# Transposing q and k by DMA from the seventh unit on, in an attention and feed-forward kernel

## The chip, the cores and the metric

The kernel runs on one core of a Trainium2 chip. The metric is the device time of one execution in microseconds. Before the change the median of three runs is 475.96 us (475.83 to 476.86). The profile is of one execution of its own.

The core's engines run side by side, each through its own list of instructions in order: TensorE (PE; PEld is its weight load), VectorE (DVE), ScalarE (ACT), GpSimd (POOL) and SyncE (SP). SyncE only issues transfers here (SPq is its queue of them); POOL casts, and issues the stores of results while attention runs. TensorE writes into PSUM, of which this kernel uses all banks; the other engines copy from there into SBUF.

## The reference

Eight batches of twelve heads, 448 tokens, head size 64; then a gated feed-forward block over 3584 tokens. All in float32; the kernel casts to bf16 (q, k) and f16 (the rest) on the chip.

```python
scores = scale * np.matmul(q, k.transpose(0, 1, 3, 2)) - np.log(S)
attn = 1.0 / (1.0 + np.exp(-scores))
attn_out = np.matmul(attn, v)                       # (8, 12, 448, 64)
x = attn_out.transpose(0, 2, 1, 3).reshape(B * S, H * D)   # (3584, 768)
g = x @ w_gate                                      # 768 -> 1536
silu = g * (1.0 / (1.0 + np.exp(-g)))
return (silu * (x @ w_val)) @ w_out                 # 1536 -> 768
```

## The kernel before, in words

**Units.** A unit is four heads of one batch: 24 units, three to a batch, numbered i from 0; b = i // 3. A unit has two head pairs (pp = 0, 1), and a pair fills the 128 partitions with two heads of 64. Of the 448 tokens, 384 are the main part, loaded as 128 partitions of three tokens (s = 0, 1, 2; NS = 3); the last 64 are the tail, loaded for a whole batch at once.

**One unit, step by step.** (1) SyncE loads q, k and v of the four heads (`load_main`, L239; 393 KB each) and, per batch, the tails (`tails_batch`, L214 and L225). The tails of q and k share a buffer sqk, q in one half of the partitions and k in the other, which half is which alternating by batch. (2) POOL casts them (`cast_main`, `cast_tails`, L199; value tails to vbd, L276). (3) TensorE transposes, for each pair, three blocks of k, three of q and one of the tails, each 128x128, into one PSUM bank (`tr`, L336 and L338); VectorE copies 832 columns of it to qkT (L342) and the k tail in two 64x64 blocks onto the diagonal of a zeroed 128x128 buffer kbd (L348). (4) Scores: `burst` (L362) takes two (pair, chunk) steps of four matmuls; `burst_tail` (L376) takes the key tails of both heads of a pair in one matmul, which is why the k tail has to be block-diagonal. (5) ScalarE takes the sigmoid (L385). (6) `pv` (L398, L400) multiplies by v; VectorE copies the result to xT (L405), which is already the transposed input of the feed-forward block.

**Feed-forward.** Per batch, `f1` makes twelve gate and value blocks: six matmuls for ps_g, six for ps_v (L424), with the sigmoid on ScalarE (L430) and two products on VectorE (L434 writes t and frees the bank of ps_g, L440 writes hT). ps_g and ps_v share two PSUM banks (tag "G"). Per pair of batches `f2` makes the output, twelve matmuls to a block (L472, ps_o; ps_ol at the end). The transposes of `tr` and the blocks of `f2` share one PSUM bank (tag "TO").

**Order.** The main loop (L560 on) lists operations in the order in which the work should be preferred: in round i the loads of unit i+3, the casts of unit i+2, in four slices the scores of unit i and the transposes of unit i+1 (slices 1 and 2), between them `f1` and `f2`. Each carries an engine, an assumed duration, its inputs and the buffer slots that it takes and gives back. `list_schedule` (L47) then plays the list through: an engine that is free takes the first operation of a window of its own list (40 for PE, 8 for POOL, 1 for SP) whose inputs and slots are there, by the assumed times. What it finds is emitted in order of its start times, so every engine's order on the chip is fixed. The chip then waits by semaphores, by its own times. The weights are loaded in rounds 0 to 4: twelve loads of w_out last (L308), cast on POOL (L313); staging buffers (tag "st") are ten for all loads.

The lines on which the change bears most:

```python
    slots = {"A": 2, "TO": 1, "P": 1, "G": 2, "st": 10, "sqk": 2, "sv": 2, "q16": 2, "k16": 2, "qk16": 2,
             "v16": 3, "qkT": 4, "pt": 10, "xT": 14, "osb": 2}
...
        a = op("PE", 0.41, fpe, deps=casts_of(i, pp), take=["TO"], give=[x for o in casts_of(i, 0) for x in o.take] if pp else [])
        m = op("DVE", 0.59, fm, deps=[a], take=["qkT"])
        kd = op("DVE", 0.4, fk, deps=[a, m, R.get(("sct", i - 2))], give=a.take)
```

Of the kernel before, what the change touches and what calls it, by code (L numbers as in the profile page):

```python
# [125 lines left out]
def kernel(  # L126
# [17 lines left out]
    SM = 384  # L144
# [16 lines left out]
    slots = {"A": 2, "TO": 1, "P": 1, "G": 2, "st": 10, "sqk": 2, "sv": 2, "q16": 2, "k16": 2, "qk16": 2,  # L161
             "v16": 3, "qkT": 4, "pt": 10, "xT": 14, "osb": 2}
# [4 lines left out]
    NKB = 4  # L167
    kbd = [one.tile([128, 128], BF16, tag=f"kbd{i}", name=f"kbd{i}") for i in range(NKB)]
# [5 lines left out]
    for t in kbd:  # L174
        nc.vector.memset(t, 0.0)
# [29 lines left out]
    def tails_batch(b):  # L205
        def load_qk():
            T["sqk", b] = stg.tile([128, H, D], FP32, tag="sqk", bufs=2, name=f"sqk{b}")
        lo, hi = (q, k) if b % 2 == 0 else (k, q)

        def part(src, sl, first):  # L210
            def fn():
                if first:
                    load_qk()
                nc.sync.dma_start(out=T["sqk", b][sl],  # L214
                                  in_=src[b][:, SM:S, :].rearrange("h p d -> p h d"))
            return fn
        a = op("SP", 0.6, part(lo, slice(0, 64), True), take=["sqk"], nbytes=64 * H * D * 4)
        c = op("SP", 0.6, part(hi, slice(64, 128), False), deps=[], nbytes=64 * H * D * 4)
        R["sqk", b] = [a, c]

        def vpart(hp):
            def fn():
                if hp == 0:
                    T["sv", b] = stg.tile([128, H // 2, D], FP32, tag="sv", bufs=2, name=f"sv{b}")
                nc.sync.dma_start(out=T["sv", b][64 * hp:64 * hp + 64],  # L225
                                  in_=v[b][hp:H:2, SM:S, :].rearrange("h p d -> p h d"))
            return fn
        R["sv", b] = [op("SP", 0.6, vpart(0), take=["sv"], nbytes=64 * H // 2 * D * 4),
                      op("SP", 0.6, vpart(1), nbytes=64 * H // 2 * D * 4)]
# [16 lines left out]
    def cast_main(i, nm, eng, dt, part=None):  # L246
        def fn():
            if part in (None, 0):
                T[nm, i] = sb.tile([128, NS, 4, D], dt, tag=nm, bufs=slots["v16"] if nm == "v16" else 2,
                                   name=f"{nm}_{i}")  # L250
            h0, h1 = (0, 4) if part is None else (2 * part, 2 * part + 2)
            src = T["st_" + nm[0], i][:, h0:h1].rearrange("p h s d -> p s h d")
            cp(eng, T[nm, i][:, :, h0:h1, :], src)
        n = 4 if part is None else 2
        take = []
        if part in (None, 0):
            take = [nm]
        last = part in (None, 1)
        R[nm, i, part] = op(eng, 0.05 + n * 0.2, fn, deps=[R["st_" + nm[0], i, part]], take=take,
                            give=(R.get(("st_" + nm[0], i, None)) or R["st_" + nm[0], i, 0]).take if last else [])  # L260

    def cast_tails(i, eng="POOL"):
        b, r = divmod(i, QB)

        def fqk():
            T["qk16", i] = sb.tile([128, 4, D], BF16, tag="qk16", bufs=2, name=f"qk16_{i}")
            cp(eng, T["qk16", i], T["sqk", b][:, 4 * r:4 * r + 4, :])
        R["qk16", i] = op(eng, 0.4, fqk, deps=R["sqk", b], take=["qk16"], give=R["sqk", b][0].take if r == QB - 1 else [])
# [48 lines left out]
    def casts_of(i, pp):  # L317
        o = [R["qk16", i]]
        for nm in ("q16", "k16"):
# [346 lines left out]
```

## Time and profile before

| | |
|---|---|
| median of three runs | 475.96 us |
| profiled execution | 474.18 us, span 472.0 us |
| TensorE busy | 451.4 us (96%), 2832 matmuls |
| VectorE, ScalarE, POOL busy | 205.1 us (43%), 221.9 us (47%), 120.5 us (26%) |
| granted TensorE clock | 0.991 on average |
| transposes | 336 matmuls of 128x128 (L336: 288, L338: 48) |
| transfers | 58.66 MB, mean 124 GB/s; the queue of SP 51.13 MB, that of POOL 7.08 MB |

A row of the timeline or of the chain gives the start and the length in microseconds from the span's start, the engine, the line, and what is written from what; in square brackets stands how long the engine was idle before it and which event ended that. A row of the groups gives the count, then the total busy time and the mean nanoseconds of one, then the idle time just before. In a row of windows stand the stretch and its length, the busy time (and number of instructions) of PE, PEld, DVE, ACT and POOL, then the granted clock, the share of the DMA engines' time and the rate in GB/s. Matmuls are pipelined: the lengths of successive ones overlap, so that what one costs is read from the starts.

### The profile page before, as it was taken

Reading aid. Unit: us, or ns where it says so; the run is one execution under the profiler, and the core shown is the slowest. Engines: PE = TensorE matmul, PEld = TensorE weight load, DVE = VectorE, ACT = ScalarE, POOL = GpSimd, SP = SyncE. Lnnn points to the kernel's source line nnn. Section 1 sums busy time; section 2 is a strip of 40 time slices with the busy share of each in tenths; the row PEclk is TensorE's granted clock in tenths of the full one; section 3 lists DMA queues with packets and bytes.
Section 4 is the critical chain, followed back from the end, with each engine's and each line's share of the span. In section 5 each row is a group of like instructions: output and inputs, shape, how many; then the busy total and the mean of one; then the engine's idle time right before and its main releaser. Section 6 shows DMA issues by size and latency. Waiting matters only on the chain.

```text
span 472.0 us, 7257 instructions
## 1 busy us (share of the span) xinstructions
PE 451.4 (96%) x2832; PEld 224.0 (47%) x2832; DVE 205.1 (43%) x422; ACT 221.9 (47%) x296; POOL 120.5 (26%) x207
## 2 busy tenths in 40 slices
PE   2778999999999999999999999999999999999996
PEld 1323444444555545545455455454554544554563
DVE  2333655555544444444344453444544443335211
ACT  3577666656445354453554455445545344121111
POOL 4758768431211123121321232112210000000000
PEclk9979999999999999999999999999999999999999
DMA  8999999989413253332541323000000001110032
GB/s 213 347 300 357 320 334 365 235 224 293 120 34 102 67 135 78 93 115 69 134 126 60 101 72 96 0 35 35 33 28 7 35 35 33 55 47 0 35 101 100
DMA packets 68385, 58.66 MB, mean 124 GB/s; under 512 B 21248, under 2 KB 64512, under 8 KB 68352
## 3 DMA queue, kind: packets, MB, share of 16 engines
q1 hardware_dynamic: 66864, 51.13, 37.3%
q0 software_dynamic: 1488, 7.08, 4.2%
q8 instruction: 22, 0.36, 0.3%
q14 instruction: 11, 0.09, 0.1%
HBM read 47.19 MB, written 11.01 MB: 123 GB/s over the span
## 4 chain that ended last, share of the span: by engine, by line
PE 88%; DMA 7%; SPq 1%; DVE 1%; ACT 1%; POOL 0%; issue 0%
PE ps_g L424 23%; PE ps_v L424 22%; PE ps_o L472 18%; PE ps_sc L362 6%; PE ps_pv L398 6%; PE ps_ol L472 5%; PE ps_tr L336 3%; PE ps_pv L400 3%; DMA st_v<-in_v_dram 3%; DMA st_k<-in_k_dram 2%; DMA st_wv<-in_moe_w_val_dram 2%; PE ps_sct L376 2%; DVE t L434 1%; SPq L239 1%; ACT s L430 1%; PE ps_tr L338 0%
## 5 line engine op out<-in xcount | busy, mean ns | idle before, releaser
L385 ACT ACTIVATE pt<-ps_sc,sbiast 128x896 f16<-128x896 f32 x144 | 136.8, 1006 | 34.1 <-PE ps_sc L362 34.1
L424 PE MATMUL ps_g<-xT,wg 128*128 128x448 f16 x576 | 124.6, 352 | 1.1 <-DVE t L434 1.1
L424 PE MATMUL ps_v<-xT,wv 128*128 128x448 f16 x576 | 124.8, 353 | 0.0
L430 ACT ACTIVATE s<-ps_g 128x448 f16<-128x448 f32 x96 | 52.2, 544 | 146.6 <-PE ps_g L424 146.4
L434 DVE TENSOR_TENSOR t<-ps_g,s 128x448 f16<-128x448 f32 x96 | 59.9, 624 | 117.7 <-ACT s L430 117.7
L472 PE MATMUL ps_o<-wo,hT 128*128 128x384 f16 x516 | 90.9, 326 | 0.0
L472 PEld LDWEIGHTS <-hT 128*128 128x128 f16 x672 | 65.6, 98 | 45.8 <-issue 0.7
L424 PEld LDWEIGHTS <-wg 128*128 128x128 f16 x576 | 55.7, 98 | 53.3 <-issue 4.4
L440 DVE SCALAR_TENSOR_TENSOR hT<-ps_v,t 128x448 f16<-128x448 f32 x96 | 60.0, 625 | 43.3 <-PE ps_v L424 40.0
L424 PEld LDWEIGHTS <-wv 128*128 128x128 f16 x576 | 54.0, 98 | 45.8 <-issue 4.4
L405 DVE CAST xT<-ps_pv 128x448 f16<-128x448 f32 x48 | 29.9, 624 | 38.5 <-PE ps_pv L400 38.5
L362 PE MATMUL ps_sc<-qkT 64*128 64x448 bf16 x288 | 42.3, 369 | 4.3 <-ACT pt L385 3.6
L398 PE MATMUL ps_pv<-pt,v 128*64 128x448 f16 x288 | 37.8, 370 | 0.0
L199 POOL CAST v<-st_v 128x768 f16<-128x768 f32 (+1 forms) x25 | 20.2, 808 | 67.8 <-PE ps_pv L398 63.0
L497 POOL DMA_DIRECT2D out_dram<-osb x15 | 8.3, 556 | 100.0 <-DVE osb L485 53.0
L199 POOL CAST q<-st_q 128x768 bf16<-128x768 f32 x23 | 19.0, 825 | 58.2 <-issue 50.7
L342 DVE COPY qkT<-ps_tr 128x832 bf16<-128x832 bf16 x48 | 27.9, 582 | 11.5 <-PE ps_tr L338 11.5
L483 ACT ACTIVATE osb<-ps_o 128x384 f32<-128x384 f32 x22 | 10.8, 491 | 40.7 <-PE ps_o L472 40.7
L472 PE MATMUL ps_ol<-wo,hT 128*128 128x384 f16 x156 | 26.8, 326 | 0.0
L385 ACT ACTIVATE pt<-ps_sct,sbiast 128x896 f16<-128x896 f32 x24 | 24.1, 1003 | 4.2 <-PE ps_sct L376 4.1
L336 PE MATMUL ps_tr<-idn,k 128*128 128x128 bf16 x144 | 17.2, 233 | 8.6 <-ACT k L195 4.4
L485 DVE TENSOR_SCALAR osb<-ps_o 128x384 f32<-128x384 f32 x21 | 11.7, 558 | 27.3 <-PE ps_o L472 27.3
(36 smaller groups left out, 223.2 us busy)
## 6 DMA issues: line engine op xcount, KB each, us to landing
st_q<-in_q_dram SPq DMA_DIRECT2D x23, 384.0 KB, 4.8
st_k<-in_k_dram SPq DMA_DIRECT2D x23, 384.0 KB, 5.4
st_v<-in_v_dram SPq DMA_DIRECT2D x23, 384.0 KB, 6.3
out_dram<-osb POOLq DMA_DIRECT2D x15, 384.0 KB, 2.6
st_wg<-in_moe_w_gate_dram SPq DMA_DIRECT2D x12, 384.0 KB, 7.4
st_wv<-in_moe_w_val_dram SPq DMA_DIRECT2D x12, 384.0 KB, 8.5
st_wo<-in_moe_w_out_dram SPq DMA_DIRECT2D x12, 384.0 KB, 8.7
out_dram<-osb SPq DMA_DIRECT2D x8, 384.0 KB, 2.3
```

The source lines that it names most:

```text
L199: nc.gpsimd.tensor_copy(out=o, in_=i)
L336: nc.tensor.transpose(out=ps[:, off + s * 128:off + (s + 1) * 128], in_=src[:, s, hs, :], identity=idn)
L342: nc.vector.tensor_copy(out=m, in_=T["tr", i, pp][:, mo:mo + S + SM])
L362: nc.tensor.matmul(out=sc[:, hp, 0:S], lhsT=kT[r, s * 128:(s + 1) * 128], rhs=qT[r, :], start=True, stop=True)
L385: nc.scalar.activation(out=pt, in_=T[("sc",) + key][:, :, 0:S], func=SIGM, bias=sb_t, scale=qkscale)
L398: nc.tensor.matmul(out=ps[c, :], lhsT=T["v16", i][:, s, 2 * pp + hp, :], rhs=T["pt", i, pp, s][:, hp, :], start=(s == 0), stop=False)
L405: nc.vector.tensor_copy(out=t, in_=T["pv", i, pp])
L424: nc.tensor.matmul(out=ps, lhsT=w[c][:, j, ff * 128:(ff + 1) * 128], rhs=T["xT", b, j], start=(j == 0), stop=(j == KC - 1))
L430: nc.scalar.activation(out=t, in_=T["g", b, f], func=SIGM)
L434: nc.vector.tensor_tensor(out=t, in0=T["g", b, f], in1=T["s16", b, f], op=MULT)
L440: nc.vector.scalar_tensor_tensor(out=T["hT", m, f][:, o * S:(o + 1) * S], in0=T["v", b, f], scalar=HSC, in1=T["t1", b, f], op0=MULT, op1=MULT)
L472: nc.tensor.matmul(out=o, lhsT=T["hT", m, f][:, t * 128:(t + 1) * 128], rhs=wo16[f][:, cs], start=(f == 0), stop=(f == NF - 1))
```

## The change

The bf16 copies of q, k and their tails go into one buffer `src16` of two slots, 128 partitions x 2 pairs x 8 blocks x 128 columns: three blocks of k, a block of k tail, and four blocks of q with its tail (the tail first in odd batches). The k tail is written as two 64x64 pieces on the diagonal of its block, into a buffer zeroed once at the start, so that the transposed block is the block-diagonal key of `burst_tail`; kbd and its copies go. For that the k tails are loaded like the value tails, each head in its own half of the partitions, and a batch's tails take five loads where they took four. Each cast of q and k is of one pair (128x384) instead of both.

Units 0 to 5 are still transposed on TensorE: eight blocks a pair, then one VectorE copy of 1024 columns. From unit 6 (NPE = 6) `tr_dma` issues one transposing DMA from SyncE for the whole unit, SBUF to SBUF, 128 x 2048 bf16 into qkT as 16 transposed blocks. It is listed in round i, slice 2, for unit i+2. The planner is told 2.1 us on SP and 800000 bytes for it. qkT has three slots of a whole unit instead of four of a pair, given back by the unit's last `burst`. v is cast without reordering.

```diff
-    slots = {"A": 2, "TO": 1, "P": 1, "G": 2, "st": 10, "sqk": 2, "sv": 2, "q16": 2, "k16": 2, "qk16": 2,
-             "v16": 3, "qkT": 4, "pt": 10, "xT": 14, "osb": 2}
+    slots = {"A": 2, "TO": 1, "P": 1, "G": 2, "st": 10, "sq": 2, "sk": 2, "sv": 2, "src": 2,
+             "v16": 3, "qkT": 3, "pt": 10, "xT": 14, "osb": 2}
...
+    NSRC = slots["src"]
+    src16 = [one.tile([128, 2, 8, 128], BF16, tag=f"src{i}", name=f"src{i}") for i in range(NSRC)]
...
-    for t in kbd:
+    for t in src16:
         nc.vector.memset(t, 0.0)
...
+        for nm, src in (("sk", k), ("sv", v)):
+            R[nm, b] = [op("SP", 0.6, part(nm, src, 0), take=[nm], nbytes=64 * H // 2 * D * 4),
+                        op("SP", 0.6, part(nm, src, 1), nbytes=64 * H // 2 * D * 4)]
...
+    def cast_qk(i, nm, pp, eng):
+        g = groups(i // QB, nm)[0]
+
+        def fn():
+            o = src16[i % NSRC][:, pp, g:g + NS, :].rearrange("p s (h d) -> p s h d", h=2)
+            cp(eng, o, T["st_" + nm, i][:, 2 * pp:2 * pp + 2].rearrange("p h s d -> p s h d"))
...
+        R["c" + nm, i, pp] = op(eng, 0.43, fn, deps=[ld], take=["src"] if nm == "q" and pp == 0 else [],
+                                give=ld0.take if pp else [])
...
+        def fk():
+            for hp in range(2):
+                ps = slice(64 * hp, 64 * hp + 64)
+                cp(eng, src16[i % NSRC][ps, :, gk, ps], T["sk", b][ps, 2 * r:2 * r + 2, :])
...
+    def tr_pe(i, pp):
+
+        def fpe():
+            ps = T["tr", i, pp] = psum.tile([128, 8 * 128], BF16, tag="TO", bufs=1, name="ps_tr")
+            for g in range(8):
+                nc.tensor.transpose(out=ps[:, g * 128:(g + 1) * 128],
+                                    in_=src16[i % NSRC][:, pp, g, :], identity=idn)
...
+    def tr_dma(i):
+
+        def fn():
+            qkT_tile(i)
+            nc.sync.dma_start_transpose(
+                out=T["qkT", i].rearrange("p a (g c) -> p (a g) c", c=128),
+                in_=src16[i % NSRC].rearrange("p a g c -> p (a g c)"))
+        d = op("SP", 2.1, fn, deps=[R["c" + nm, i, pp] for nm in "qk" for pp in range(2)] + R["tails", i],
+               take=["qkT"], give=R["cq", i, 0].take, nbytes=800000)
+        R["qkT", i, 0] = R["qkT", i, 1] = d
...
     def casts(i):
-        cast_main(i, "q16", "POOL", BF16)
-        cast_main(i, "k16", "POOL", BF16)
+        for nm in "qk":
+            for pp in range(2):
+                cast_qk(i, nm, pp, "POOL")
         cast_tails(i)
-        cast_main(i, "v16", "POOL", FP16)
+        cast_v(i, "POOL")
         cast_vtail(i)
...
-                        if i + 1 < NQ:
-                            tr(i + 1, 0)
+                        if i + 1 < NPE:
+                            tr_pe(i + 1, 0)
...
+            if att and sl == 2 and NPE <= i + 2 < NQ:
+                tr_dma(i + 2)
```

Three places show how the order of the instructions moves. The first is on TensorE in the long middle of the kernel, behind the tail scores of a unit. Before (k_13, q_13 and qk_13 are the casts of unit 13):

```order
L376 LDWEIGHTS kbd_73
L376 MATMUL ps_sct<-qkT_1_2196,kbd_73 128x448
L336 LDWEIGHTS k_13_1949
L336 MATMUL ps_tr<-idn,k_13_1949 128x128
...
L336 MATMUL ps_tr<-idn,q_13_1943 128x128
...
L338 MATMUL ps_tr<-idn,qk_13_1964 128x128
L424 LDWEIGHTS wv_0_96
L424 MATMUL ps_v<-xT_0_1787,wv_0_96 128x448
```

Now:

```order
L392 LDWEIGHTS qkT_1858
L392 MATMUL ps_sct<-qkT_1858 128x448
L439 LDWEIGHTS wv_1_93
L439 MATMUL ps_v<-xT_0_1687,wv_1_93 128x448
L439 MATMUL ps_v<-xT_1_1733,wv_1_93 128x448
```

Three transposes of k, three of q and one of the tails have gone from between the tail scores and the value matmuls; the same goes for the second group of each unit. TensorE has 96 transposes in all where it had 336.

The second is on TensorE behind unit 5 (v_5), where the first unit transposed by DMA is read (qkT_987). The xT tiles up to xT_5_525 (before) and xT_5_512 (now) belong to batch 0, xT_0_642 to xT_5_1028 to batch 1. Before, one gate and one value group stand between the last scores of unit 5 (qkT_1_797) and the first of unit 6 (qkT_0_921):

```order
L362 MATMUL ps_sc<-qkT_1_797 128x448
L424 LDWEIGHTS wg_2_94
L424 MATMUL ps_g<-xT_0_279,wg_2_94 128x448
...
L424 MATMUL ps_v<-xT_5_525,wv_2_98 128x448
L362 LDWEIGHTS qkT_0_921
L362 MATMUL ps_sc<-qkT_0_921 128x448
L398 LDWEIGHTS v_5_717
L398 MATMUL ps_pv<-pt,v_5_717 64x448
```

Now:

```order
L413 MATMUL ps_pv<-pt,v_5_708 64x448
L415 MATMUL ps_pv<-pt,vbd_76 128x448
...
L439 MATMUL ps_v<-xT_0_256,wv_3_95 128x448
...
L439 MATMUL ps_g<-xT_5_512,wg_3_91 128x448
...
L439 MATMUL ps_v<-xT_5_512,wv_3_95 128x448
L439 LDWEIGHTS wg_0_88
L439 MATMUL ps_g<-xT_0_642,wg_0_88 128x448
...
L439 MATMUL ps_g<-xT_5_1028,wg_0_88 128x448
L377 LDWEIGHTS qkT_987
L377 MATMUL ps_sc<-qkT_987 128x448
```

Between the last ps_pv of unit 5, which stood behind the scores of unit 6, and those scores there are now four value groups and four gate groups on end. From the tail scores of unit 5 to the first scores of unit 6 TensorE's order is: one ps_sct, then seven pairs of value and gate groups, and between them two groups of scores and two ps_pv groups.

The third is SyncE at the end of the weight loads. Before (sqk and sv are tails, st_q, st_k and st_v the units' main loads):

```order
L308 DMA st_wo_990<-in_moe_w_out_dram 128x768
L308 DMA st_wo_1008<-in_moe_w_out_dram 128x768
L239 DMA st_q_1015<-in_q_dram 128x4x192
L239 DMA st_k_1028<-in_k_dram 128x4x192
L239 DMA st_v_1052<-in_v_dram 128x4x192
L214 DMA sqk_1063<-in_k_dram 64x12x64
```

Now:

```order
L324 DMA st_wo_958<-in_moe_w_out_dram 128x768
L324 DMA st_wo_973<-in_moe_w_out_dram 128x768
L357 DMA_TRANSPOSE qkT_987<-src_72 128x16x128
L231 DMA st_q_1013<-in_q_dram 128x4x192
L231 DMA st_k_1018<-in_k_dram 128x4x192
L231 DMA st_v_1032<-in_v_dram 128x4x192
L357 DMA_TRANSPOSE qkT_1036<-src_73 128x16x128
L209 DMA sq_1060<-in_q_dram 64x12x64
```

The transpose of unit 6 stands behind the twelfth load of w_out, ahead of the main loads of unit 8; that of unit 7 behind those. From there on one transpose stands ahead of the main loads of each following unit.

On POOL the q and k tails of a unit (406 ns a unit before, cast whenever they were there, often before q) now stand behind the two q casts, and the k tails of most units behind the two k casts.

150 lines of the change are left out of this document (65 added, 85 removed).

## The prediction

> **What bounds the kernel now.** I read the windows first (busy time of each engine by stretch), because an average over 472 us hides the stages; then TensorE's timeline, then the waits and transfers around the place where the first transposing DMA would stand.
>
> ```profile
> core 0: us, PE busy (x) PEld busy (x) DVE busy (x) ACT busy (x) POOL busy (x), PEclk, DMA share, GB/s
> 30.00:42.00 12.00, 9.54 (x53) 3.90 (x53) 3.62 (x9) 8.20 (x10) 8.98 (x13) 0.72 1.08 357
> 60.00:80.00 20.00, 20.00 (x134) 9.08 (x133) 10.47 (x22) 13.86 (x19) 14.34 (x24) 1.00 1.04 362
> 140.00:380.00 240.00, 240.00 (x1542) 120.80 (x1540) 109.84 (x224) 117.77 (x158) 46.16 (x84) 1.00 0.24 70
> 420.00:441.00 21.00, 19.91 (x101) 9.70 (x100) 9.99 (x16) 4.35 (x8) 0.00 (x0) 1.00 0.05 20
> ```
>
> There are three stages. Up to about 42 us TensorE waits for data (9.54 of 12 us busy). From 42 us TensorE has no gap, while VectorE and ScalarE are busy under half of the long stretch (110 and 118 of 240 us); until about 106 us the transfers are saturated too (share 1.04). So after 42 us a microsecond less on TensorE is a microsecond off the end, unless something new makes it wait. Where it transposes, it does this:
>
> ```profile
> 219.65 0.54 PE L376 MATMUL ps_sct<-qkT,kbd 128*128 128x448 bf16 x2
> 220.03 0.33 PE L336 MATMUL ps_tr<-idn,k 128*128 128x128 bf16 x3
> 220.20 0.33 PE L336 MATMUL ps_tr<-idn,q 128*128 128x128 bf16 x3
> 220.37 0.22 PE L338 MATMUL ps_tr<-idn,qk 128*128 128x128 bf16 x1
> 220.42 1.30 PE L424 MATMUL ps_v<-xT,wv 128*128 128x448 f16 x6
> ```
>
> Starts, not durations, give the cost, since matmuls overlap: 220.42 - 220.03 = 0.39 us for seven transposes, 0.056 us each.
>
> **Term 1, the transposes removed.** Units 6 to 23 are 18 units of two groups: 36 x 0.39 = 14.04 us off TensorE. (The Trainium skill, "TensorE: Matmul & The Clock Gate", Part 4, gives about 275 ns for one transpose within a kernel; by that 252 of them would be worth 69 us. The starts above say 0.056 us, and the sum goes by them.) VectorE loses the copies behind them, an engine with cover: nothing.
>
> **Term 2, one more transpose a group in units 0 to 5.** Eight where there were seven: 12 x 0.056 = +0.67 us, charged in full though part of it falls in the idle first 42 us.
>
> **Term 3, two-buffer stalls.** While the planner waits for the first transposed unit it pulls feed-forward work (ps_g, then ps_v) ahead, and in the new order three more gate products follow a gate/value pair with nothing between. Such a neighbourhood is at the end of the profile now:
>
> ```profile
> 420.34 1.30 PE L424 MATMUL ps_g<-xT,wg 128*128 128x448 f16 x6
> 422.93 1.29 PE L424 MATMUL ps_g<-xT,wg 128*128 128x448 f16 x6 [0.16 <-DVE t L434]
> 42.46 1.14 PE ps_v L424 x6
> ```
>
> A pair then takes 422.93 - 420.34 = 2.59 us, where two groups of 1.14 (third row, from the chain of waits) take 2.28: the gate waits for VectorE's t to free its bank. 3 x 0.31 = +0.93 us.
>
> **Term 4, POOL in the first 42 us.** POOL's casts are cut in halves, and the tails are cast after q rather than beforehand.
>
> ```profile
> L199 POOL CAST q<-st_q 128x768 bf16<-128x768 f32 x23 | 19.0, 825 | 58.2 <-issue 50.7 <-DMA st_q<-in_q_dram 6.9 <-DVE qkT L342 0.4
> L199 POOL CAST k<-st_k 128x384 bf16<-128x384 f32 x1 | 0.5, 510 | 0.0
> L199 POOL CAST qk<-sqk 128x256 bf16<-128x256 f32 x23 | 9.3, 406 | 8.7 <-DMA sqk<-in_k_dram 5.7 <-PE ps_sc L362 1.5 <-PE ps_g L424 0.8
> L276 POOL CAST vbd<-sv 64x128 f16<-64x128 f32 x48 | 14.0, 292 | 2.2 <-DMA sv<-in_v_dram 0.9
> ```
>
> A unit's q, k and tails cost 825 + 825 + 406 = 2.06 us now; then 4 x 0.51 + 0.41 (a q tail of 256 elements) + 2 x 0.29 (two k tails of 128) = 3.03 us: about +1 us a unit. After 42 us POOL has room for that (14.3 of 20 us busy, and a unit takes over 11). Before, TensorE waits for just these casts:
>
> ```profile
> 39.85 0.83 POOL L199 CAST q<-st_q 128x768 bf16<-128x768 f32 x1 [0.38 <-DMA st_q<-in_q_dram]
> 41.01 0.83 POOL L199 CAST k<-st_k 128x768 bf16<-128x768 f32 x1 [0.33 <-DMA st_k<-in_k_dram]
> 41.90 0.34 PE L336 MATMUL ps_tr<-idn,k 128*128 128x128 bf16 x3
> 53.03 0.54 PE L376 MATMUL ps_sct<-qkT,kbd 128*128 128x448 bf16 x2
> ```
>
> Unit 4 by the new order: q halves and q tail 39.85 + 1.02 + 0.41 = 41.3, k halves to 42.3, k tails to 42.9. TensorE, which would start these transposes at 41.90, starts at 42.9, but has moved a group of scores (0.49 us) ahead: it loses about 0.6. I take +0.7 (bounds: 0, if the transfer and not POOL is late, and 2, one microsecond each for units 3 and 4).
>
> **At no cost: zeroing and one more load.** The zeroed buffers grow from 64 columns (of four bytes) to 1024:
>
> ```profile
> L175 DVE MEMSET kbd<- 128x64 uint32 x4 | 0.3, 112 | 0.8 <-PEq L650 0.8
> L177 DVE MEMSET vbd<- 128x128 uint32 x3 | 0.4, 165 | 0.0
> 3.23 0.42 DVE L197 CAST q<-st_q 128x384 bf16<-128x384 f32 x1 [1.65 <-DMA st_q<-in_q_dram]
> ```
>
> By 0.83 ns a column (165 less 112 over 64) each takes 0.9 us, two 1.8; with the three of vbd VectorE is done at about 3.1 us, and the first load lets it begin at 3.23. If that cover is short, the start is late by the rest, a few tenths. A batch's tails take five loads instead of four, one more issue of about 0.63 us on SyncE (the tail row in term 5), within its slack.
>
> **Term 5, the first transposing DMA.** Unit 6 stands on SyncE behind the last w_out load, and TensorE's new order reaches its scores with no slack planned. When is it there, and when does TensorE ask?
>
> ```profile
> 64.63 0.54 PE L376 MATMUL ps_sct<-qkT,kbd 128*128 128x448 bf16 x2
> 68.76 5.18 SPq L308 DMA_DIRECT2D st_wo<-in_moe_w_out_dram x6
> 80.05 3.19 POOL L313 CAST wo<-st_wo 128x768 f16<-128x768 f32 x4
> 83.64 0.83 POOL L199 CAST q<-st_q 128x768 bf16<-128x768 f32 x1 [0.41 <-DMA st_q<-in_q_dram]
> ```
>
> TensorE: unit 5's tail scores (ps_sct) start at 64.63; add 0.7 (term 4) and four longer groups since unit 3 (0.22): 65.5. From there the new order has seven gate/value pairs (15.96), one ps_sct (0.38), two score groups (0.98), two ps_pv groups (1.96) and term 3 (0.93): it asks at **85.8 us**. The transfer: the last w_out load is there when its cast starts at about 82.4, and the load behind it landed at 83.6. In that load's place the transpose lands at 82.4 + X, X being its service time. It moves 128 x 2048 bf16 = 524 KB in 256-byte pieces.
>
> ```profile
> 171.00:172.00 1.00, 1.00 (x9) 0.44 (x9) 0.56 (x1) 0.00 (x0) 0.00 (x0) 1.00 1.08 362
> 173.00:174.00 1.00, 1.00 (x7) 0.49 (x5) 0.62 (x1) 0.00 (x0) 0.00 (x0) 1.00 1.37 167
> L214 SPq DMA_DIRECT2D sqk<-in_k_dram x2: 612/628/644, 170.2 to 229.1; - x2
> DMA to landing us min/median/max: 6.3/6.4/6.6
> ```
>
> No row shows a transposing DMA. Lower bound: the best rate of plain loads, 362 GB/s: X = 1.45 us. Nearest row: the tail loads, whose pieces are 256 bytes too, 167 GB/s: X = 3.1. Upper bound: a tail load of 197 KB takes 6.4 us from issue to landing; scaled by bytes (2.67), X = 17. I take 3.1, for the equal piece: landing at 85.5, before 85.8. Stall 0; it would be X - 3.4 us for a larger X.
>
> After unit 6 the slack grows: TensorE takes about 11.6 us a unit (53.03 to 64.63), then nearly 20 (from the ps_sct below, at 199.93, to the one at 219.65). A transpose waits for the buffer that the scores of three units earlier leave, so it may start nearly two units ahead: 20 to 35 us to spare. Behind it on SyncE wait the loads of q, k and v two units on; they have those two units. On POOL the casts two units on now wait for this transfer, since there are two source buffers; behind them stand that unit's v and value tails, which are read a unit later still.
>
> ```profile
> 199.93 0.54 PE L376 MATMUL ps_sct<-qkT,kbd 128*128 128x448 bf16 x2
> ```
>
> **The sum.** -14.04 + 0.67 + 0.93 + 0.7 + 0 = -11.7 us. The profiled execution took 474.18 us (span 472.0 and 2.2 around it) and would take 462.4; the median of the runs shown is 475.96, and minus 11.7 gives **464.2 us**.
>
> **The rivals.** (a) *Transposes of middling speed*, X from 4 to 8 us: only the saturated stretch suffers, TensorE stalls 0.6 to 5 us at units 6 to 10, and the end is at 465 to 469 us. For it: transposed writes have no row at all. Against: 256-byte pieces already run at 167 GB/s.
>
> (b) *Slow transposes, the other side*: each holds the transfers so long that units fall due faster than they arrive. Unit 10 is the fifth: it lands at 82.4 + 5X plus twelve main loads and a set of tails between (5.3 MB at 362 GB/s, 14.7), that is 97.1 + 5X, and is asked for at 85.8 + 4 x 11.6 = 132.2. The stall, 5X - 35, eats the gain of 11.7 from X = 9.4 on. At the upper bound, 17, a unit costs 17 + 3.8 us of transfers, so unit 23 lands at 82.4 + 17 + 17 x 20.8 = 453, and 89 us of work follow its first scores, which start at 382.92 in a span of 472.0:
>
> ```profile
> 382.92 0.55 PE L362 MATMUL ps_sc<-qkT 64*128 64x448 bf16 x4
> ```
>
> That is 542 us, or 544 with what lies around the span. For it: the tail loads' landing time; against: that time is mostly waiting behind two plain loads issued just before. (The Trainium skill, "VectorE: DVE Perf Modes", section "The three transpose paths", gives 1309 ns for one 128x128 block by DMA against 390 by TensorE, which speaks against this change: sixteen blocks one after another would be an estimated 21 us, and the chain above then ends near 615 us. No run here shows it yet; if blocks overlap, the figure is a latency and no rate.)
>
> (c) *The start costs more*: POOL, 9 of 12 us busy before 42 us, frees staging buffers later, loads start later, and TensorE's gapless run begins 3 to 6 us later: 467 to 470 us.
>
> (d) *It does not do what it says*: TensorE's freed time turns into waits for ScalarE or VectorE, and the time stays at 476. Both under half busy over 240 us speak against it.
>
> **How the numbers follow.** Forecast 0.62, (a) 0.16, (c) 0.08, (b) 0.11, (d) 0.03. The measurement can tell 0.2%, about 1 us, from no change. Faster are the forecast, (a) and (c): 0.86; same is (d): 0.03; slower is (b): 0.11. The range: below, 461.5, all of term 1 and little of the others; above, 470, where (a) and (c) end; (b) and (d) stay outside. The forecast alone: 462 to 466.
>
> **What would show it.** In the changed profile: transposes by DMA landing 2 to 5 us after their issue where transfers are idle; TensorE's windows from 140 us on still full, with no L336 rows; TensorE's idle time before unit 6's scores below 1 us; the first gapless window starting less than 1.5 us later. What would make it wrong: a landing time over 9 us, a TensorE wait for qkT that recurs from unit to unit, or a start that moves by more than 3 us.

## The result, and the profile after

The changed kernel takes **464.4 us** in the median of four runs (463.3 to 465.1) beside 475.9 of the kernel before on the same chip, a ratio of **0.976 (0.973 to 0.978)**. Run again beside later experiments it took 462.4 us, 0.974 (0.971 to 0.976). Forecast were 464.2 us and a range of 461.5 to 470. The profiled execution took 463.31 us, with a span of 461.2.

The windows of the changed kernel, in the stretches shown of before (the last one 11 us earlier, since the end has moved):

```profile
30.00:42.00 12.00, 8.03 (x42) 3.27 (x38) 2.63 (x4) 5.97 (x7) 8.93 (x16) 0.59 1.04 338
60.00:80.00 20.00, 20.00 (x123) 8.72 (x121) 10.36 (x17) 12.55 (x16) 14.14 (x27) 1.00 0.99 301
140.00:380.00 240.00, 240.00 (x1421) 116.01 (x1419) 93.76 (x152) 121.26 (x164) 51.76 (x117) 1.00 0.40 105
409.00:430.00 21.00, 19.91 (x102) 9.63 (x99) 9.98 (x17) 4.35 (x8) 0.00 (x0) 1.00 0.05 20
```

The long stretch is as full as before, with 1421 matmuls where there were 1542: TensorE's freed time did not turn into waits. The transfers' share there rose from 0.24 to 0.40. Only the first row is worse: 8.03 us busy of 12 where it was 9.54.

TensorE's timeline behind the tail scores of a unit has no transposes any more, and the value product follows at once:

```profile
197.13 0.54 PE L392 MATMUL ps_sct<-qkT 128*128 128x448 bf16 x2
197.51 1.30 PE L439 MATMUL ps_v<-xT,wv 128*128 128x448 f16 x6
```

The transposing DMAs, by their line, first between 75 and 130 us, then from 135 us on (nanoseconds of the issue on SyncE, least, median and most; then microseconds from the issue to the landing). The eighteenth lies between, at 131.16: it holds SyncE for 2.82 us and lands after 4.3.

```profile
L357 SPq DMA_TRANSPOSE qkT<-src x6: 4211/4586/6834, 78.9 to 122.8; - x6
DMA to landing us min/median/max: 6.3/6.9/8.8
...
L357 SPq DMA_TRANSPOSE qkT<-src x11: 1778/1981/3180, 148.1 to 331.4; - x11
DMA to landing us min/median/max: 4.3/4.3/4.9
```

Where transfers are idle, sixteen blocks are in place 4.3 us after the issue, which is at most 0.27 us a block. (The Trainium skill, "VectorE: DVE Perf Modes", section "The three transpose paths", gives 1309 ns for one block by DMA. As a rate the trace disagrees, with at most 270 ns a block for a whole unit in one instruction: its blocks overlap, or each takes less. One block alone was not measured here.)

**A clock inside the program.** Where the tail scores of unit 5 start splits the program well. These rows are of the changed kernel, then of the same kernel run again:

```profile
67.71 0.54 PE L392 MATMUL ps_sct<-qkT 128*128 128x448 bf16 x2
```

```profile
67.36 0.54 PE L392 MATMUL ps_sct<-qkT 128*128 128x448 bf16 x2
```

From there to the end it is 461.2 - 67.71 = 393.5 us, and 461.0 - 67.36 = 393.6 in the second execution. Five experiments below that alter tail loads and casts, of later batches too, and leave TensorE's order behind the point as it is, have 393.4 to 393.5. The kernel before has 472.0 - 64.63 = 407.4, and the experiment that alters only its loads 407.5. So in these traces the part behind it differs by 0.2 us at most, and nearly all the scatter of the runs is in the beginning. The span of every timed execution is known. If the constant holds in all of them, span less constant gives where the point lay in each, with far more executions than there are traces (the bounds are two standard errors; the twenty are of the changed kernel, in two sets of four, and of three experiments with the same beginning, each with its own constant):

| executions | unit 5's tail scores start at | rest |
|---|---|---|
| 47 of the kernel before | 65.4 +- 0.2 us | 407.4 |
| 20 with the changed kernel's beginning | 67.7 +- 0.5 us | 393.5 (changed kernel) |

The change in two numbers: **-13.9 us** behind that point and **+2.3 us** ahead of it. The second is less sure than its bound says. The changed kernel alone lies at 68.7 in its first four executions and at 66.7 +- 0.7 in the four run beside later experiments, while the kernel before stays within 65.2 to 65.6 in each of its four sets; and the experiment with four transposes a unit, which begins in the same way and is not among the twenty, lies at 69.0.

One rival can be tested on these executions. The granted clock in the window from 30 to 42 us fell too, from 0.72 to 0.59, and a slower TensorE would also start later. But at like clocks the gap stays: where the clock averages 0.99 or more over the span, the point lies at 65.3 (40 of the 47) and at 67.3 (10 of the 20); where it is lower, at 66.0 and 68.1.

The experiments take the two numbers apart.

### The profile page after: what moved, and what is told of

The parts are those of the page before. It is cut to its first block, busy times and chain, and to the rows that moved or that the text cites. A ratio compares the mean times of both kernels' runs of the same rounds, so it can differ in the third digit from the quotient of the medians.

```text
span 461.2 us, 6749 instructions
## 1 busy us (share of the span) xinstructions
PE 437.8 (95%) x2592; PEld 211.4 (46%) x2592; DVE 177.1 (38%) x290; ACT 221.1 (48%) x296; POOL 139.4 (30%) x299
## 4 chain that ended last, share of the span: by engine, by line
PE 87%; DMA 4%; SPq 4%; DVE 1%; ACT 1%; POOL 1%; issue 1%; POOLq 0%
PE ps_g L439 24%; PE ps_v L439 22%; PE ps_o L487 18%; PE ps_sc L377 6%; PE ps_pv L413 6%; PE ps_ol L487 5%; PE ps_pv L415 3%; SPq L216 2%; DMA st_wv<-in_moe_w_val_dram 2%; SPq L231 2%; PE ps_sct L392 2%; DMA st_v<-in_v_dram 2%; DVE t L449 1%; ACT s L445 1%; POOL src L199 1%; DMA st_q<-in_q_dram 1%
## 5 line engine op out<-in xcount | busy, mean ns | idle before, releaser
L199 POOL CAST src<-st_q 128x384 bf16<-128x384 f32 x46 | 22.0, 505 | 46.9 <-DMA st_q<-in_q_dram 41.9
L199 POOL CAST src<-st_k 128x384 bf16<-128x384 f32 x47 | 22.5, 506 | 6.2 <-DMA st_k<-in_k_dram 5.0
L377 PEld LDWEIGHTS <-qkT 64*128 64x128 bf16 x288 | 9.1, 95 | 32.5 <-issue 30.5
L500 DVE TENSOR_SCALAR osb<-ps_o 128x384 f32<-128x384 f32 x21 | 11.7, 558 | 30.7 <-PE ps_o L487 30.7
```

The costliest lines, as they stand in the source:

```text
L199: nc.gpsimd.tensor_copy(out=o, in_=i)
L377: nc.tensor.matmul(out=sc[:, hp, 0:S], lhsT=kT[r, s * 128:(s + 1) * 128], rhs=qT[r, :], start=True, stop=True)
L500: nc.vector.tensor_scalar_mul(T["osb", m, t][:, c], o, HREC)
```

## The experiments

### Where the gain is: transposes back on TensorE

**All units on TensorE.** The buffers, loads and casts of the changed kernel, without any transposing DMA.

```diff
-    NPE = 6
+    NPE = 24
```

> All 24 units are transposed on TensorE, from the same source buffer and with the same casts and loads as in the changed kernel; no transposing DMA. Theory A (the gain is TensorE's time for the transposes, 8 x 0.056 us a group): 36 groups x 0.45 = 16 us more than the changed kernel's 464.4, less up to 0.9 for the three two-buffer stalls that the old order does not have: 479.5 to 480.4, that is slower than the kernel before. Rival B (the gain comes from what went with the transposes: VectorE's diagonal copies, the free PSUM bank, the new layout): 464 to 470.

479.3 us, 1.009 (1.007 to 1.012): slower than the kernel before, as theory A has it. By the point above: 477.5 - 68.15 = 409.4 us behind it, 15.9 more than with DMAs from unit 6 on, or 0.44 us for each of 36 groups of eight. Rival B falls for the new layout and the missing diagonal copies, which stay here: the part behind the point is 2.0 us longer than in the kernel before, and 36 more transposes of 0.057 us make 2.0. The PSUM bank is taken again in this run, so it does not test what a free bank brings; the sums of starts further below leave about 0.5 us for that and all else.

**Units 6 to 11 on TensorE.**

```diff
-    NPE = 6
+    NPE = 12
```

> Units 6 to 11 go back to TensorE, units 12 to 23 stay with transposing DMAs, so that none stands in the saturated stretch. Theory A: 12 groups x 0.45 = 5.4 us more, less 0.9 if the three stalls at unit 6 go away: 468.8 to 469.8. Rival C (the transposes in the saturated stretch cost something that the trace does not show as a wait, 1 to 3 us): 466 to 468.

467.6 us, 0.984 (0.981 to 0.987), a little under what A expected (468.8), and within rival C's figures too; the time alone does not decide. The trace does: 464.5 - 66.14 = 398.4 us behind the point, 4.9 more than 393.5. A's 5.4 less what the three stalls cost (0.96, below) is 4.5. By C it would be another 1 to 3 us less, and it is 0.4 more, so C falls.

### How far the transposes are from costing something

**Each transpose issued twice.** The added one writes a buffer that nobody reads; the other engines' orders stay.

```diff
             qkT_tile(i)
+            nc.sync.dma_start_transpose(out=scr.rearrange(...), in_=src16[i % NSRC].rearrange(...))
             nc.sync.dma_start_transpose(
```

> Every transposing DMA is issued twice, first into a scratch buffer that nobody reads, then into qkT; the order on every other engine stays. Theory S (a transpose costs its transfer, X about 1.7 to 3 us, with slack after unit 6): X doubles to 3.4 to 6, TensorE stalls 2 to 4 us at unit 6 and no more after unit 10: 464 to 468. Rival Q (it costs the time that SyncE is held by the issue, 6.8 us for the first and 4.2 for the next five while transfers are saturated): unit 6 about 6.5 us late, units 7 to 10 fall behind by another 1 to 2 us each: 471 to 477. The prediction's formula for slow transposes, 5X - 35, gives a loss only from X = 7 on.

464.9 us, 0.978 (0.974 to 0.981), as theory S has it. SyncE's timeline, and TensorE's wait at unit 6:

```profile
77.11 6.90 SPq L359 DMA_TRANSPOSE scr<-src  x1
84.12 1.58 SPq L362 DMA_TRANSPOSE qkT<-src  x1
...
88.51 0.55 PE L382 MATMUL ps_sc<-qkT 64*128 64x448 bf16 x4 [1.68 <-DMA qkT<-src]
```

The first transpose holds SyncE for 6.9 us, the second, right behind it, for 1.58. So the long issue is a wait behind the saturated transfers and no price of the instruction; at the next four units the second ones take 1.86 to 2.86 us. A second one adds its transfer, and TensorE waits 1.68 us. Rival Q falls. The unit takes 1.6 us more and nothing is lost after it (461.5 - 66.41 = 395.1 behind the point, 1.6 over 393.5).

**Each transpose issued four times**, three of them into one buffer, so that each waits for the last to land.

```diff
+            for x in range(3):
+                nc.sync.dma_start_transpose(out=scr.rearrange(...), in_=src16[i % NSRC].rearrange(...))
```

> Every transposing DMA is issued four times, three of them into one scratch buffer, so that each of these waits for the one before to land (4.3 us or more): X about 16 us a unit. By the formula of the prediction's slow case: unit 23's transpose lands at 82.4 + 16 + 17 x (16 + 3.8) = 435, the end comes 89 us later, 524 us and 2 around the span: 526, within 20. If the slow case does not exist (SyncE and the transfers have room for four): below 480.

540.3 us, 1.137 (1.133 to 1.140). The slow case exists, 14 us further out than expected. The formula's stall at unit 10 was 5 x 16 - 35 = 45 us. Its tail scores start at 182.48 here and at 139.87 in the changed kernel; less the 1.4 us by which this execution began later (its unit 5 at 69.07), the stall is 41 us. The real transposes are issued from 94.64 to 423.42 us, 19.3 us apart (assumed 19.8); with the X of 15.5 that this gives, the formula's stall is 43.

```profile
94.64 2.57 SPq L362 DMA_TRANSPOSE qkT<-src  x1
...
423.42 3.07 SPq L362 DMA_TRANSPOSE qkT<-src  x1
```

What the formula lacked is seen in the windows and in the row of busy times:

```profile
90.00:140.00 50.00, 28.05 (x139) 11.19 (x141) 11.24 (x18) 17.23 (x23) 7.73 (x18) 0.78 0.89 180
380.00:440.00 60.00, 60.00 (x356) 29.03 (x354) 23.47 (x38) 30.27 (x42) 11.55 (x26) 1.00 0.77 158
```

```profile
PE 452.3 (84%) x2592; PEld 214.6 (40%) x2592; DVE 177.1 (33%) x290; ACT 221.2 (41%) x296; POOL 138.5 (26%) x299
```

The last transposes no longer set the end: TensorE is without a gap from 380 us, still working off what it had waited for. And in the stretch where it waits, its granted clock is lower (0.78, with 28 of 50 us busy): the same 2592 matmuls are busy for 452.3 us, against 437.8 in the changed kernel. How the 14 us divide between the two is not worked out.

**DMA from unit 3 on.**

```diff
-    NPE = 6
+    NPE = 3
```

> Units 3, 4 and 5 are transposed by DMA too. Theory A alone (TensorE's time): 6 groups x 0.45 = 2.7 us less than the changed kernel, 460 to 462. If a transpose in the saturated stretch holds SyncE for 4 to 7 us and the loads behind it as long: units 3 to 6 each start 4 to 7 us later than they could, of which the freed 0.9 us a unit pays little: 470 to 485, with TensorE waiting for loads and qkT between 30 and 90 us.

472.6 us, 0.996 (0.993 to 0.999): most of the gain is gone, as the second theory has it. Its transposes up to 95 us, and the first wait for one:

```profile
L357 SPq DMA_TRANSPOSE qkT<-src x5: 4225/7130/8118, 42.5 to 94.9; - x5
DMA to landing us min/median/max: 6.3/9.7/11.7
...
51.73 0.55 PE L377 MATMUL ps_sc<-qkT 64*128 64x448 bf16 x4 [3.47 <-DMA qkT<-src]
```

The first ones hold SyncE for over 7 us while weights and the next units' loads stand behind. TensorE is busy 13.64 of 18 us from 42 to 60 us, and 14.59 of 20 from 80 to 100. Unit 3's tail scores come 13 us later than in the changed kernel (56.15 for 42.99), of which the order makes up some later. Transfers are saturated here as they are for units 6 to 10. That these three units are not covered because TensorE has little other work so early is argued from the order, and no run tests it.

### What the start lost

POOL casts of unit 3's q and TensorE's first transposes behind them, in the changed kernel (the rows of POOL, then TensorE's):

```profile
30.62 0.95 POOL L199 CAST src<-st_q 128x384 bf16<-128x384 f32 x2 [0.60 <-DMA st_q<-in_q_dram]
31.64 0.40 POOL L199 CAST src<-sq 64x256 bf16<-64x256 f32 x1
32.10 0.64 POOL L199 CAST src<-sk 64x128 bf16<-64x128 f32 x2
33.15 0.95 POOL L199 CAST src<-st_k 128x384 bf16<-128x384 f32 x2 [0.41 <-POOL src L199]
...
33.71 1.03 PE L341 MATMUL ps_tr<-idn,src 128*128 128x128 bf16 x8 [2.54 <-POOL src L199]
```

The same place in the kernel before:

```profile
28.82 0.82 POOL L199 CAST q<-st_q 128x768 bf16<-128x768 f32 x1 [0.84 <-DMA st_q<-in_q_dram]
29.94 0.83 POOL L199 CAST k<-st_k 128x768 bf16<-128x768 f32 x1 [0.30 <-DMA st_k<-in_k_dram]
...
30.83 0.50 PE L336 MATMUL ps_tr<-idn,k 128*128 128x128 bf16 x3 [0.80 <-POOL k L199]
```

The transposes are 2.9 us later for two reasons: q arrives 1.8 us later, and from its cast to the transposes it is 3.1 us where it was 2.0. The second is POOL, foreseen in term 4. The first is a load, and in both kernels POOL waits for it. What makes the loads late? SyncE's timeline of the changed kernel has the tails of the second batch as follows, and issues unit 3's q at 26.64 (23.71 before):

```profile
18.39 0.61 SPq L209 DMA_DIRECT2D sq<-in_q_dram  x1
19.58 3.23 SPq L216 DMA_DIRECT2D sk<-in_k_dram  x2
22.85 3.69 SPq L216 DMA_DIRECT2D sv<-in_v_dram  x2
26.64 0.56 SPq L231 DMA_DIRECT2D st_q<-in_q_dram  x1
```

I had two theories: the one more load (H1), or that q and one half of k now share half of the partitions (H2).

**Tails of q and k loaded as before**, k's cast from its half onto both diagonal blocks.

```diff
-        for nm, src in (("sk", k), ("sv", v)):
+        def kpart():
+            r = slice(64, 128) if b % 2 == 0 else slice(0, 64)
+            nc.sync.dma_start(out=T["sq", b][r], in_=k[b][:, SM:S, :].rearrange("h p d -> p h d"))
...
-                cp(eng, src16[i % NSRC][ps, :, gk, ps], T["sk", b][ps, 2 * r:2 * r + 2, :])
+                kr = slice(64, 128) if b % 2 == 0 else slice(0, 64)
+                cp(eng, src16[i % NSRC][ps, :, gk, ps], T["sq", b][kr, 4 * r + hp:4 * r + 4:2, :])
```

> The tails of q and k are loaded as in the kernel before (one buffer, q in one half of the partitions, k in the other, four loads a batch); the k tails are cast from that half onto both diagonal blocks, with the same number of casts. POOL's work stays. Theory H2 (the 2.9 us that the start lost come from tail loads that put three quarters of the bytes of q's and k's tails into one half of the partitions): the start comes back by 2.5 to 2.9 us, unit 3's tail scores near 40.2 instead of 42.99, time 461.5 to 462. Theory H1 (they come from the one more load that SyncE issues, 0.63 us each): 463.1 to 463.8. POOL theory (term 4 of the prediction): 464.4, start unchanged.

462.3 us, 0.973 (0.971 to 0.976). The time lies between what H2 and H1 wrote down and decides nothing: both were reckoned from 464.4, and the changed kernel itself took 462.4 when it was run again (below). Unit 3's q is cast at 29.61, 1.0 us earlier, and the point behind unit 5 lies at 66.8 +- 0.7 over five executions, 0.9 us (0 to 1.8) earlier than the 67.7 of the table. Unit 3's tail scores start at 40.92, where six traces with the changed kernel's beginning have 41.60 to 43.26. By the point H2's 2.5 to 2.9 us do not come; it is near H1 (0.6 to 1.3).

**The kernel before, with k's tail in two loads** into the same half.

```diff
-        c = op("SP", 0.6, part(hi, slice(64, 128), False), deps=[], nbytes=64 * H * D * 4)
-        R["sqk", b] = [a, c]
+        R["sqk", b] = [a] + [op("SP", 0.6, half(hi, slice(64, 128), h0), nbytes=64 * H // 2 * D * 4)
+                             for h0 in (0, H // 2)]
```

> The kernel before with one edit: the k tail of a batch is loaded in two loads of six heads, into the same half of the partitions as before, so five tail loads a batch as in the changed kernel, but the halves stay even. H2: the start moves by 0.2 to 0.8 us, time 476.0 to 476.8. H1: the start moves by 2 to 3 us as in the changed kernel, 478 to 479.

476.1 us, 1.003 (1.001 to 1.004); the point lies at 66.6 +- 0.3 over twelve executions, 1.2 us later than in the kernel before, more than one issue of 0.63 us and less than H1 wrote down. The time alone lies in H2's range, but only because the kernel before took 474.7 us beside this run and not 475.96. H2's mechanism falls: the halves are even here, and unit 3's q is issued at 26.47 all the same. What one more load does shows in the windows from 4 to 12 us, behind the first batch's tails. First the kernel before, then with its k tail split, then the changed kernel, then with four tail loads again:

```profile
4.00:12.00 8.00, 3.34 (x19) 1.56 (x19) 2.28 (x7) 2.29 (x3) 4.24 (x12) 1.00 1.14 268
```

```profile
4.00:12.00 8.00, 3.00 (x19) 1.56 (x19) 1.60 (x5) 2.42 (x3) 3.53 (x10) 1.00 0.91 240
```

```profile
4.00:12.00 8.00, 2.46 (x16) 1.14 (x17) 2.01 (x6) 2.42 (x3) 1.90 (x5) 1.00 0.90 232
```

```profile
4.00:12.00 8.00, 3.38 (x21) 1.69 (x21) 2.15 (x6) 2.38 (x3) 2.63 (x7) 1.00 1.13 278
```

With four tail loads the transfers are saturated (share 1.14 and 1.13); with five they are not (0.91 and 0.90), although the bytes and the 256-byte pieces are the same and loads stand waiting on SyncE. The other traces agree: 0.91 to 0.99 in seven more with five loads, 1.13 or 1.14 in three with three. Eight microseconds at 30 GB/s less are a quarter of a megabyte, 0.7 us of full rate. The second batch does it once more, less clearly: from 24 to 30 us the share is 1.21 in the kernel before and 0.92 with its k tail split, but over all traces 0.91 to 1.18 with five and 1.06 to 1.21 with fewer. That splitting one load in two leaves the transfers unfilled is shown; by which limit, is not.

**The changed kernel again**, as a base on the same chip.

> The changed kernel once more, as the base for the three beside it and for the spread of its start: 0.974 to 0.977 of the kernel before; unit 5's tail scores between 66.0 and 68.2 us, since three executions with the same beginning had them at 66.14, 67.71 and 68.15 (64.63 before).

462.4 us, 0.974 (0.971 to 0.976), unit 5's tail scores at 67.36: as expected. Over its four executions the point lies at 66.7 +- 0.7; the next three experiments were run beside it.

**k of units 3 to 5 cast on VectorE.** TensorE's order stays.

```diff
-            cp(eng, o, T["st_" + nm, i]...
+            cp("DVE" if nm == "k" and 3 <= i < 6 else eng, o, T["st_" + nm, i]...
```

> The changed kernel with the k casts of units 3, 4 and 5 on VectorE instead of POOL (TensorE's order is the same), which takes 0.95 us of each unit off POOL's chain from q's arrival to the transposes. POOL part of the lost start (from the q cast to the transposes 3.1 us now, 2.0 before): unit 3's transposes start 2.0 to 2.2 us after its q cast, the gapless run about 1 us earlier, 0.8 to 1.5 us less than the changed kernel. Loads alone (theory H1, the fifth tail load): no change within 0.5 us, since the loads arrive as late as before.

462.2 us, 0.972 (0.970 to 0.975), within the 0.5 us of the base that loads alone allow. Its trace shows what the edit did:

```profile
30.71 0.95 POOL L199 CAST src<-st_q 128x384 bf16<-128x384 f32 x2 [1.64 <-DMA st_q<-in_q_dram]
...
32.49 1.11 PE L341 MATMUL ps_tr<-idn,src 128*128 128x128 bf16 x8 [1.79 <-DVE src L197]
```

q arrives as late as in the changed kernel (30.71), and from its cast to the transposes it is 1.8 us instead of 3.1. The point lies at 66.3 +- 0.9 over five executions, 1.4 us (0.4 to 2.4) earlier than the 67.7 of the table, but only 0.4 earlier than in the base beside it. So POOL's chain is shorter by what was taken off it; that the end gains by that is likely, and this run alone does not show it.

**Three tail loads**: as with four, and v's tail in one load.

```diff
-            R[nm, b] = [op("SP", 0.6, part(nm, src, 0), ...), op("SP", 0.6, part(nm, src, 1), ...)]
+            T["sv", b] = stg.tile([64, H, D], FP32, tag="sv", bufs=2, name=f"sv{b}")
+            nc.sync.dma_start(out=T["sv", b], in_=v[b][:, SM:S, :].rearrange("h p d -> p h d"))
...
-                                      in_=T["sv", b][ps, 2 * r:2 * r + 2, :])
+                                      in_=T["sv", b][:, 4 * r + hp:4 * r + 4:2, :])
```

> As the run with q's and k's tails in one buffer (four tail loads), and v's tails also in one load of 197 KB instead of two of 98 KB, cast to both diagonal blocks: three tail loads a batch, the same bytes in the same 256-byte pieces. If small loads are what leaves the transfers idle (share 0.77 to 0.97 from 4 to 12 us with five loads, 1.03 to 1.23 with four), the loads of unit 3 come another 1 to 2 us earlier: 1.5 to 3 us less than the changed kernel. If only the move from four to five loads costs: 0.8 to 1.3 us less than the changed kernel.

462.3 us, 0.973 (0.971 to 0.975). Unit 3's q is issued at 21.84, three microseconds earlier than with four loads, and cast at 29.54, no earlier (29.61); the point lies at 66.6 +- 0.7, as with four loads (66.8), 1.1 us earlier than the 67.7 of the table and 0.1 earlier than in the base beside it. The 1.5 to 3 us of the first theory do not come: once the transfers are saturated, an earlier issue waits in them. The 0.8 to 1.3 us of the second fit the table and not the base.

**Three loads and k on VectorE.**

> Both edits together, three tail loads a batch and the k casts of units 3 to 5 on VectorE. If load and POOL parts add up: 2.5 to 4 us less than the changed kernel, 0.967 to 0.971 of the kernel before. If one hides the other: no better than the better of the two alone.

460.9 us, 0.971 (0.969 to 0.974): the ratio is at the upper end of what was expected if the two parts add, but it is 1.5 us less than the base and not 2.5 to 4. The point lies at 65.6 +- 0.6 us, 2.1 earlier than the 67.7 of the table (1.1 and 1.4 for each edit alone) and 1.1 (0.2 to 2.0) earlier than the base beside it (0.1 and 0.4 alone). So the two edits together do bring the start forward; that their parts simply add is not shown.

**v's tail behind the main loads**, in addition.

```diff
             loads(i + 3)
+            if (i + 3) % QB == 0:
+                vtail_load((i + 3) // QB)
```

> As the run with three tail loads and the k casts of units 3 to 5 on VectorE, with v's tail load moved behind the main loads of the same unit. If the slow transfer of the tails (about 180 GB/s around 25 us) is what unit 3's q waits for once SyncE no longer is: unit 3's q cast starts about 1 us earlier than there (29.90), 28.5 to 29, and the time is 0.5 to 1.5 us below it: 0.968 to 0.971. If the start is set by something else (ScalarE, the weights' casts): q cast earlier but time within 0.3 us of that run, 0.971 to 0.972.

460.8 us, 0.970 (0.969 to 0.972); the point at 65.2 +- 0.6. q is cast 1.9 us earlier, but the transposes begin at 31.53, hardly before those of the run above (31.71), since now k comes last:

```profile
28.05 0.96 POOL L199 CAST src<-st_q 128x384 bf16<-128x384 f32 x2 [2.47 <-DMA st_q<-in_q_dram]
...
30.92 1.01 DVE L197 CAST src<-st_k 128x384 bf16<-128x384 f32 x2 [4.57 <-DMA st_k<-in_k_dram]
...
31.53 0.62 PE L349 MATMUL ps_tr<-idn,src 128*128 128x128 bf16 x8 [2.14 <-DVE src L197]
```

By time this move is worth nothing that can be told. But the start is back where it was before the change (65.2 against 65.4), with the 13.9 us behind it kept. This version beats the kernel before clearly; against the changed kernel (0.974 in the run beside the others) the intervals of the time touch, while the start's (2.5 us earlier than the 67.7 of the table, bounds 0.6 and 0.5) are apart.

## Why the prediction was right, step by step

The sum came out at -11.7 us and the measured difference is -13.9 + 2.3 = -11.6. That the two agree so closely is luck. There are two errors in it that nearly cancel: the start cost about 1 us more than charged, and the rest brought 0.8 us more. The mechanism was right, and without the luck the time would still lie in the range.

**What bounds the kernel**: right. After 42 us a microsecond less on TensorE was one off the end, and in the experiments with NPE = 12 and 24 a microsecond more was one more.

**Terms 1 and 3** together were to be -14.04 + 0.93 = -13.1 us behind unit 5's tail scores; it is -13.9. The starts carried the price of a transpose well: 36 x 0.446 = 16.1 us was to come back with all units on TensorE, and 15.9 did. Where the 0.8 us come from can be added up from the two traces, by the time from each matmul's start to the next one's, summed over all behind the point:

| us behind the point | before | changed | difference |
|---|---|---|---|
| transposes (252 before) | 14.30 | 0 | -14.30 |
| ps_g and ps_v | 209.90 | 211.91 | +2.01 |
| ps_o and ps_ol | 114.84 | 113.49 | -1.35 |
| scores and ps_pv | 68.34 | 68.09 | -0.25 |

The transposes took 14.30 us, 0.0567 each, where 14.04 were charged. Term 3 is in the trace at the forecast place, three gates in a row of the changed kernel, behind a pair that does not wait:

```profile
79.08 1.30 PE L439 MATMUL ps_g<-xT,wg 128*128 128x448 f16 x6
80.22 1.30 PE L439 MATMUL ps_v<-xT,wv 128*128 128x448 f16 x6
81.67 1.29 PE L439 MATMUL ps_g<-xT,wg 128*128 128x448 f16 x6 [0.16 <-DVE t L449]
...
84.26 1.29 PE L439 MATMUL ps_g<-xT,wg 128*128 128x448 f16 x6 [0.16 <-DVE t L449]
...
86.84 1.30 PE L439 MATMUL ps_g<-xT,wg 128*128 128x448 f16 x6 [0.16 <-DVE t L449]
...
88.07 0.55 PE L377 MATMUL ps_sc<-qkT 64*128 64x448 bf16 x4
```

Pairs are 2.59 us apart, as taken from the end of the profile before. The idle time shown in each is 0.16 us, but the price is read from the starts: from ps_v to the waiting ps_g it is 1.45 us and not 1.14. By starts each of these stalls costs 0.32 us in both traces, and there are 10 where there were 7: 0.96 us, where 0.93 were charged. So term 3 was right, and term 1 was 0.26 us too small. The other 0.5 us of the 0.8 lie in which groups of matmuls now follow each other, which no term had. (The 275 ns of the Trainium skill, "TensorE: Matmul & The Clock Gate", Part 4, is no price in this stream: by it the 288 transposes of the experiment would have cost an estimated 79 us, and they cost 15.9.)

**Term 2 and term 4** were +0.67 and +0.7 us, nearly all ahead of the point: 1.4. It is 2.3 +- 0.5. Term 4's mechanism is in the trace, about 1 us more from q's arrival to the transposes. How the 2.3 us divide is not shown. If the load of the next paragraph costs here the 1.2 that it costs in the kernel before, 1.1 or so is left for POOL, as much as its chain grew, and more than the 0.7 charged. Taking k's casts away, which shortens the chain a little below what it was before, gives 1.4 us back against the table (0.4 to 2.4) and 0.4 against the base beside it; only with the load taken away too is it clear of the base's noise. The term counted the group of scores moved ahead as a relief of 0.4 us for unit 4, and left unit 3 out of its value (its upper bound has it).

**At no cost: one more load** is the step that was wrong. It was put down to one issue of 0.63 us "within its slack". In the first 30 us there was no slack for it, and it cost more than the issue: one more load took the transfers' share from 1.14 to 0.91 and cost 1.2 us (0.8 to 1.6) in the kernel before. The zeroing was nearly hidden, as forecast: VectorE's memsets take 0.91 us each and end at 3.43, its first cast starts at 3.48 where it was 3.23, and the first scores come 0.2 us later (8.61 for 8.37).

**Term 5** was right, with a margin thinner than it looks. TensorE was to ask at 85.8 and the transfer to land at 85.5. With the start 2 us later both moved: the last w_out cast starts at 86.00, the transpose lands at 78.86 + 8.8 = 87.7, so X = 1.7 us, near the lower bound (1.45) and not the 3.1 taken; TensorE begins unit 6's scores at 88.07, 0.1 us after it could. From unit 5's tail scores to them it is 20.36 us, forecast 20.3. A transpose added in front costs 1.68 us: X once more, and no cover left at this unit.

**The rivals.** (a) and (d) did not come: X is under 4, and the long stretch stayed full. (c) did not come as it was described: the start moved by 2.3 us and not 3 to 6. For unit 3 no buffer was waited for, since SyncE issues q right behind the tails (26.54 and 26.64); in unit 4's loads its gaps grew by 0.5 us in all, which may be a little of (c). (b) did not come either, but its arithmetic was tested: at X = 16 the stall at unit 10 is 41 us where 5X - 35 gives 45.

**What would show it**: no transposes on TensorE from 140 us on and full windows, as listed; TensorE's idle time before unit 6's scores is 0.1 us. The landing of 2 to 5 us holds where transfers are idle (4.3), and not in the saturated stretch (6.3 to 8.8), which has cover. "The first gapless window starting less than 1.5 us later" was missed: by the point behind unit 5 it is 2.3.

## What to carry to other kernels

Where one engine has no gap for hundreds of microseconds, count what is taken off it by the distance of starts in its own stream; that sum came within 6% here (13.1 for 13.9 us). The short stage in front of it, where loads are saturated, is harder: there a load more was not an issue more, and it needs a price of its own. Find a point behind which the program takes a constant time, so that the scatter of the beginning can be told from the effect of an edit; and compare with a base run beside the edit, since here the base's start moved by 2.0 us between two sets of four.

## What the hardware showed that was not expected

- **Issue time that is a wait.** A transposing DMA holds SyncE for 1.8 to 3.2 us (median 2.0) where transfers are mostly idle and for 4.1 to 6.9 (up to 8.1) where they are saturated; a second one right behind the first of these takes 1.6.
- **One load split in two left the transfers unfilled.** Five tail loads of a batch instead of four, same bytes and pieces: share 0.91 instead of 1.14 over 8 us, with loads waiting on SyncE.
- **Casts on POOL across the halves of the partitions** cost what others cost: three tail casts of a unit (64x256 and two 64x128, one of these from the other half) take 1.07 us together, where they took 0.40 + 0.64 within their own halves.
- **Waiting came with a lower clock.** With four transposes a unit the granted clock was 0.78 over 50 us in which TensorE was busy for 28, and the same matmuls were busy for 452.3 us instead of 437.8.
